# Grouping the 32-column matmuls of a fused attention and gMLP kernel into fewer stretches, and reordering two loads

## The chip, the cores and the metric

The kernel runs on one core of a Trainium2 chip. The metric is the time of one execution in microseconds (us) on that core; lower is better. Three runs of the kernel before gave 208.30, 208.47 and 208.62 us, median 208.47. One further execution was taken by the hardware profiler: its own time is 208.18 us, and its span from the first to the last instruction is 206.5 us. All times inside the kernel are counted from the start of that span.

## The reference

Tokens: S = 2048, width D = 512, all data bf16. The output is the input plus two branches, both fed by the same layer norm:

```
xn  = layernorm(x)                          # over the 512 columns
out = x + attention(xn) + gmlp(xn)

attention: q, k, v = xn @ wqkv              # 32 heads of 16 columns
           logits[s, w] = q[s] . k[s - 2w] / 4,  w = 0..7, masked where s - 2w < 0
           o = softmax over w (logits) applied to v[s - 2w];  result o @ wo
gmlp:      z = gelu(xn @ w_in)              # 1376 columns, split into z1 and z2 (688 each)
           g = w_sp @ layernorm(z2) + b_sp  # w_sp is 2048 x 2048, over the tokens
           result (z1 * g) @ w_out
```

So each token attends to itself and seven earlier tokens, two apart, and the gMLP mixes over all tokens.

## The kernel before, in words

Tokens are handled in 16 tiles of 128. The order of the work on each engine is the order in which the source issues it; no scheduler moves anything. Each engine works through its own queue in order, and so does the DMA queue of SyncE (SP).

**Loads.** x arrives in four blocks of four tiles (`load_x`, L160). The pool `xqp` holds three blocks, so the fourth (L178) has to wait on SP until the four tiles of the first have been normalised. The v weights `wv` (L176) and the small `b16` (L177) are issued between blocks 2 and 3. `a_sb` (L132) is a buffer that holds the softmax weights, written first by `softmax_exp(0)`.

**Layer norm.** VectorE (DVE) computes the statistics of a tile (L185, L186) and normalises it (L190); GpSimd (POOL) does Newton steps for the root. Tiles 0 to 3 are transposed by TensorE (PE). Tiles 4 to 15 go in pairs through the loop at L387, which issues one DMA transpose for each tile (L219) on SP, into `xnT`. Five transposing loads of `w_sp` (`load_wsp`, L343) follow on SP, with `w_z1` (L421) between them.

**First matmul stage, written out by hand, L398 to L479.** Three things are interleaved on PE:
- `z2_tile(i)` (L229): 8 matmuls of 344 columns, then a Gelu on ScalarE (ACT, L234); later `z2_square(i)` on ACT (L238) for the second layer norm.
- `qk_chunk(b, c)` (L260): 8 matmuls of 512 columns for q and k, copied out by ACT (L263).
- `v_pair(d)` (L285) and `reduce_heads(hb, p)` (L310): these two use a *32-column form*. The stationary operand is 128 x 32, and four such matmuls go beside each other to four column positions of the array (`tile_position=(0, 32 * k)`). A `v_pair` is 32 of them, a `reduce_heads` is 16. All other matmuls of this stage fill the array (128 x 128).

`products(hb, p)` (L301, DVE) multiplies q with shifted k; there are two buffers `pr`, so a third product waits for the `reduce_heads` that reads the first. `reduce_heads` sums the 16 columns of each head, ACT scales the result into `lg` (L312), and `softmax_top` (DVE, L317 to L322), `softmax_exp` (ACT, L325) and `softmax_norm` (DVE, L331 to L336) follow once for each half (`hb`) of the tokens.

`z2_stats` (L244) waits for the last square; `z2_norm` (L252) normalises the 16 tiles of z2 on DVE.

A stretch of matmuls in the 32-column form between two others is called an *excursion* here. There are eight: `reduce_heads` with `v_pair` (four times, from L433, L441, L449 and L456), `v_pair(4)` to `v_pair(7)` with `reduce_heads(1, 0)` (from L469), and one `reduce_heads` alone at L519, L523 and L527.

**Mixing stage.** `mix(j)` (L493) is 32 matmuls over `w_sp` and z2; `z1_tile(j)` (L505) is 8 more with a Gelu (L510) on a tile whose padding POOL has cleared (L509); `gate_out(j)` (L515) multiplies on DVE and issues a DMA transpose of the result on SP. Each `mix(j)` also issues the load of `w_sp` for j + 5. From j = 3 on, DVE does the attention's weighted sums (L559 to L568) beside it, at set places.

**Last stage.** PE multiplies with `wo` (L636) and `w_out` (L647, L622), DVE adds x (L651), SP stores.

PSUM: `bank_pair` hands out three double banks in turn, two banks serve `ps_aux` (transposes and head sums).

Of the kernel before, what the change touches and what calls it, by code (L numbers as in the profile page):

```python
# [7 lines left out]
BF16 = mybir.dt.bfloat16  # L8
# [5 lines left out]
P = 128  # L14
S = 2048
D = 512
# [29 lines left out]
def kernel(  # L46
# [20 lines left out]
    SP = nc.sync  # L67

    x2 = A_x.rearrange("b s d -> (b s) d")
# [15 lines left out]
    def bank_pair(name, two=False):  # L85
        turn[0] += 1
        pool = ps_b if turn[0] % 3 == 0 and not two else ps_a
        return pool.tile([P, 2, 512], F32, name=name, tag="mm")
# [43 lines left out]
    a_sb = base.tile([P, W, NB * TG], BF16, name="a_sb")  # L132
# [6 lines left out]
    wv = rpool.tile([P, C, D], BF16, name="wv")  # L139
# [9 lines left out]
    xqp = early.enter_context(tc.tile_pool(name="xqp", bufs=3))  # L149
# [7 lines left out]
    wqkv_r = A_wqkv.rearrange("(k p) f -> p k f", p=P)  # L157
    xq = []

    def load_x(b):  # L160
        t = xqp.tile([P, 4, D], BF16, name="xq")
        SP.dma_start(t[:], x2[b * 4 * P:(b + 1) * 4 * P, :].rearrange("(i p) d -> p i d", p=P))
        xq.append(t)

    x0 = xqp.tile([P, 4, D], BF16, name="xq")
# [4 lines left out]
    SP.dma_start(w_z2[:, 2:4, :], w_in_r[:, 2:4, FH:F])  # L170
    xq.append(x0)
    load_x(1)
    for s in range(2):
        SP.dma_start(wqk[:, :, s, :], wqkv_r[:, :, s * D:(s + 1) * D])
    load_x(2)
    SP.dma_start(wv[:], wqkv_r[:, :, 2 * D:3 * D])  # L176
    SP.dma_start(b16[:], B_b_sp.rearrange("(j p) -> j p", p=P))  # L177
    load_x(3)  # L178
    V.memset(qk[0][:, 1, :, 0:HALO], 0.0)
    V.memset(vp[0:32, :, 0, 0:HALO], 0.0)  # L180

# [1 line left out]
    def ln_stats(i):  # L183
        xs = xq[i // 4][:, i % 4, :]
        V.bn_stats(stats[:, i, :], xs)  # L185
        V.bn_aggr(mv[:, i, :], stats[:, i, :])  # L186

    def ln_apply(i):
        xn = xnp.tile([P, D], BF16, name="xn")
        V.tensor_scalar(xn[:], xq[i // 4][:, i % 4, :], mv[:, i, 0:1], rstd[:, i:i + 1], ALU.subtract, ALU.mult)  # L190
        return xn
# [26 lines left out]
    def transpose_dma(i, xn):  # L218
        SP.dma_start_transpose(xnT[:, :, i * P:(i + 1) * P], xn[:])  # L219

    def z2_start(i):
        pz = bank_pair("pzb")
        for kc in range(C):
            z2_part(i, pz, kc)
        return pz
# [7 lines left out]
    def z2_gelu(i, pz):  # L233
        A.activation(z2[:, i, :].rearrange("p (a b) -> p a b", a=2), pz[:, :, 0:FHALF],  # L234
                     ACT.Gelu_apprx_tanh, accum_out=zsum[:, i:i + 1])

    def z2_square(i):
        A.activation(junk[:], z2[:, i, :], ACT.Square, accum_out=zsq[:, i:i + 1])  # L238

    def z2_tile(i):  # L240
        z2_gelu(i, z2_start(i))
# [13 lines left out]
    def qk_chunk(b, c):  # L255
        tsl = slice(b * 512, (b + 1) * 512)
        pq = bank_pair("pq")
        for s in range(2):
            for kc in range(C):
                PE.matmul(pq[:, s, :], wqk[:, kc, s, c * P:(c + 1) * P], xnT[:, kc, tsl],  # L260
                          start=(kc == 0), stop=(kc == C - 1))
        at = HALO + b % 2 * 512
        A.copy(qk[b // 2][:, :, c, at:at + 512], pq[:])  # L263
# [16 lines left out]
    def v_pair(d2):  # L280
        pv = bank_pair("pv")
        for dd in range(2):
            for kc in range(C):
                for k in range(NG):
                    PE.matmul(pv[32 * k:32 * k + 32, dd, :].rearrange("p (b t) -> p b t", b=NB),  # L285
                              wv_v[:, kc, 2 * d2 + dd, :], xnT_g[:, kc, :, k, :],
                              start=(kc == 0), stop=(kc == C - 1), tile_position=(0, 32 * k))
        A.copy(vp[:, 2 * d2:2 * d2 + 2, :, HALO:HALO + TG],
               pv[:].rearrange("p a (b t) -> p a b t", b=NB))

    def shifted(ap):

        return bass.AP(ap.tensor, ap.offset, [ap.ap[0], [DIL, 2]] + list(ap.ap[1:]))
# [4 lines left out]
    def products(hb, p):  # L298
        pr = prp.tile([P, 2, C, SB], BF16, name="pr")
        off = HALO - DIL * (W - 1 - 2 * p)  # L300
        V.tensor_tensor(pr[:], qk[hb][:, 0, :, HALO:HALO + SB].unsqueeze(1).broadcast_to([P, 2, C, SB]),  # L301
                        shifted(qk[hb][:, 1, :, off:off + SB]), ALU.mult)
        prs[hb, p] = pr

    def reduce_heads(hb, p):
        pr = prs.pop((hb, p))
        pl = ps_aux.tile([P, 2, TG], F32, name="pl", tag="aux")
        for c in range(C):
            for k in range(NG):
                PE.matmul(pl[32 * k:32 * k + 32, :, :], rsel[:, c, :], pr[:, :, c, k * TG:(k + 1) * TG],  # L310
                          start=(c == 0), stop=(c == C - 1), tile_position=(0, 32 * k))
        A.activation(lg[hb][:, 2 * p:2 * p + 2, :], pl[:], ACT.Copy, scale=float(DH) ** -0.5)  # L312

    def softmax_top(hb):
        l = lg[hb]
        if hb == 0:
            V.tensor_tensor(l[0:32, :, 0:HALO], l[0:32, :, 0:HALO], mask[:], ALU.add)  # L317
        m4 = lgp.tile([P, 4, TG], BF16, name="m4", bufs=1)
        V.tensor_tensor(m4[:], l[:, 0:4, :], l[:, 4:8, :], ALU.max)
        V.tensor_tensor(m4[:, 0:2, :], m4[:, 0:2, :], m4[:, 2:4, :], ALU.max)  # L320
        V.tensor_tensor(m4[:, 0, :], m4[:, 0, :], m4[:, 1, :], ALU.max)
        V.tensor_tensor(l[:], l[:], m4[:, 0, :].unsqueeze(1).broadcast_to([P, W, TG]), ALU.subtract)  # L322

    def softmax_exp(hb):
        A.activation(a_sb[:, :, hb * TG:(hb + 1) * TG], lg[hb][:], ACT.Exp)  # L325
# [15 lines left out]
    def load_wsp(j):  # L341
        t = wspp.tile([P, NT, P], BF16, name="wspT")
        SP.dma_start_transpose(t[:], B_w_sp[j * P:(j + 1) * P, :])  # L343
        wsps[j] = t
# [41 lines left out]
    prev = None  # L386
    for g in groups + (None,):  # L387
        if g:
            for i in range(*g):
                ln_stats(i)  # L390
            ln_newton(*g)
        if prev:
            for i in range(*prev):
                transpose_dma(i, ln_apply(i))
        prev = g


# [32 lines left out]
    qk_chunk(2, 1)  # L430
    z2_square(7)
    qk_chunk(2, 2)
    reduce_heads(0, 0)  # L433
    products(0, 2)
    v_pair(0)
    qk_chunk(2, 3)
    z2_tile(8)
    qk_chunk(3, 0)
    z2_square(8)
    qk_chunk(3, 1)  # L440
    reduce_heads(0, 1)  # L441
    products(0, 3)
    v_pair(1)
    qk_chunk(3, 2)
    z2_tile(9)
    qk_chunk(3, 3)
    z2_square(9)
    z2_tile(10)
    reduce_heads(0, 2)  # L449
    products(1, 0)  # L450
    v_pair(2)
    z2_square(10)
    z2_tile(11)
    z2_square(11)
    z2_tile(12)
    reduce_heads(0, 3)  # L456
    softmax_top(0)
    products(1, 1)
    v_pair(3)
    z2_square(12)  # L460
    z2_tile(13)
    z2_square(13)
# [1 line left out]
    z2_square(14)  # L464
    z2_tile(15)
    z2_square(15)


    v_pair(4)  # L469
    z2_stats()  # L470
    z2_norm()
    v_pair(5)
    reduce_heads(1, 0)
    products(1, 2)
    softmax_exp(0)
    v_pair(6)
# [12 lines left out]
    def mix(j):  # L489
        pg = bank_pair("pg", j > 3)  # L490
        for k in range(NT):
            for hh in range(2):
                PE.matmul(pg[:, hh, 0:FHALF], wsps[j][:, k, :], z2[:, k, hh * FHALF:(hh + 1) * FHALF],  # L493
                          start=(k == 0), stop=(k == NT - 1))
        gs = gsp.tile([P, 2, FHALF], BF16, name="gs")
        A.activation(gs[:], pg[:, :, 0:FHALF], ACT.Identity, bias=b_col[:, j:j + 1])  # L496
        if j + 5 < NT:
            load_wsp(j + 5)
        return gs

    def z1_tile(j, gs):
        pz = bank_pair("pz1", j > 3)
        for hh in range(2):
            for kc in range(C):
                PE.matmul(pz[:, hh, 0:FHALF], xnT[:, kc, j * P:(j + 1) * P],  # L505
                          w_z1[:, kc, hh * FHALF:(hh + 1) * FHALF],
                          start=(kc == 0), stop=(kc == C - 1))
        z1 = z1p.tile([P, FPAD], BF16, name="z1")
        G.memset(z1[:, FH:FPAD], 0.0)  # L509
        A.activation(z1[:, 0:FH].rearrange("p (a b) -> p a b", a=2), pz[:, :, 0:FHALF], ACT.Gelu_apprx_tanh)  # L510
        gate[j] = (gs, z1)

    def gate_out(j):
        gs, z1 = gate.pop(j)
        V.tensor_tensor(z1[:, 0:FH], gs[:].rearrange("p a b -> p (a b)"), z1[:, 0:FH], ALU.mult)  # L515
        SP.dma_start_transpose(uT[:, :, j * P:(j + 1) * P], z1[:])

    g0 = mix(0)
    reduce_heads(1, 1)  # L519
    products(1, 3)  # L520
    z1_tile(0, g0)
    g1 = mix(1)
    reduce_heads(1, 2)  # L523
    softmax_norm(0, lgp)
    z1_tile(1, g1)
    gate_out(0)
    reduce_heads(1, 3)  # L527
    softmax_top(1)
    gate_out(1)
    z1_tile(2, mix(2))  # L530
    softmax_exp(1)
    att.close()

# [95 lines left out]
    for pair in range(2):  # L629
# [9 lines left out]
        for jj in (2 * pair, 2 * pair + 1):  # L639
            hb, q = jj // 2, jj % 2  # L640
            for k in range(NG):
                i = 8 * hb + 2 * k + q
# [48 lines left out]
```

## Time and profile before

| what | value |
|---|---|
| median of three runs | 208.47 us |
| profiled execution, its own time | 208.18 us |
| its span | 206.5 us |
| granted clock of PE | 1.00 |
| PE matmul busy | 201.7 us (98%) |
| DVE busy | 166.2 us (81%) |
| ACT busy | 93.6 us (45%) |
| POOL busy | 16.1 us (8%) |

PE's busy time is the union of its matmuls as recorded; these overlap in the record, since the next one starts before the end of the one before is reached. So a busy PE can still hold small gaps between the starts, and the starts are what has to be read. Where the idle time of an engine is named, the last thing it waited for is named with it.

### The profile page before, as it was taken

What the parts mean: (1) busy time and instruction counts of PE and PEld (TensorE: products, weight loads), DVE (VectorE), ACT (ScalarE), POOL (GpSimd) and SP (SyncE); (2) the same over time, 40 slices, a digit from 0 to 9 for tenths busy, and PEclk for the clock granted to TensorE, in tenths of its full rate; (3) what the DMA queues carried; (4) which work ended last, traced back from release to release, by engine and by line L of the source; (5) the groups of instructions that cost most, each with busy time, mean ns of one, the idle gap of its engine ahead of it and who ended that gap; (6) DMA issues with size and microseconds to landing.
All of it is one profiled execution on the core that took longest, in us unless ns stands there. A gap on an engine that the chain in (4) does not pass through costs nothing.

```text
span 206.5 us, 4016 instructions
## 1 busy us (share of the span) xinstructions
PE 201.7 (98%) x1644; PEld 118.3 (57%) x1644; DVE 166.2 (81%) x192; ACT 93.6 (45%) x145; POOL 16.1 (8%) x82
## 2 busy tenths in 40 slices
PE   7999999999999999999999999999999999999994
PEld 4754544545556665566666666666666664444442
DVE  4899939958369699999999999999999955582353
ACT  3777887675689996328633322123333311000000
POOL 5045630000000000000000000000000000000000
PEclk9999999999999999999999999999999999999999
DMA  6996546978000004623975999999544233036432
GB/s 166 318 344 101 103 101 146 236 136 157 3 0 3 3 0 43 134 51 76 174 156 123 231 179 195 217 190 187 122 141 120 45 79 42 25 97 209 115 104 90
DMA packets 67410, 25.63 MB, mean 124 GB/s; under 512 B 57168, under 2 KB 67264, under 8 KB 67264
## 3 DMA queue, kind: packets, MB, share of 16 engines
q1 hardware_dynamic: 67008, 25.24, 57.6%
q8 instruction: 13, 0.21, 0.4%
q10 hardware_dynamic: 384, 0.13, 0.3%
q14 instruction: 5, 0.04, 0.1%
HBM read 9.79 MB, written 2.10 MB: 58 GB/s over the span
## 4 chain that ended last, share of the span: by engine, by line
PE 91%; DVE 3%; DMA 3%; POOL 1%; issue 1%
PE pg L493 36%; PE pq L260 10%; PE po L647 10%; PE pz L505 9%; PE pzb L229 8%; PE pv L285 7%; PE po L636 6%; PE pl L310 4%; DMA xnT<-xn 2%; DVE stats L185 2%; DMA xq<-in_A_x_dram 1%; PE pt L212 1%; PE po L622 1%; DVE xn L190 1%; DVE mv L186 0%
## 5 line engine op out<-in xcount | busy, mean ns | idle before, releaser
L493 PE MATMUL pg<-z,wspT 128*128 128x344 bf16 x512 | 77.3, 309 | 0.0
L493 PEld LDWEIGHTS <-wspT 128*128 128x128 bf16 x512 | 49.9, 98 | 25.2 <-issue 0.8
L301 DVE TENSOR_TENSOR pr<-qk 128x8192 bf16<-128x8192 bf16 x8 | 35.1, 4425 | 6.5 <-PE pl L310 6.5
L496 ACT ACTIVATE gs<-pg,b_col 128x688 bf16<-128x688 f32 x16 | 13.3, 834 | 54.1 <-PE pg L493 54.1
L559 DVE TENSOR_TENSOR pw<-vp,a_sb 128x4096 bf16<-128x4096 bf16 x16 | 36.1, 2285 | 0.0
L651 DVE TENSOR_TENSOR ot<-po,xr 128x512 bf16<-128x512 f32 x15 | 10.2, 689 | 15.2 <-PE po L647 15.1
L260 PE MATMUL pq<-xnT,wqk 128*128 128x512 bf16 x96 | 21.7, 379 | 0.0
L505 PE MATMUL pz<-w_z,xnT 128*128 128x344 bf16 x128 | 21.3, 309 | 0.0
L229 PE MATMUL pzb<-w_z,xnT 128*128 128x344 bf16 x128 | 20.6, 309 | 0.3 <-DMA xnT<-xn 0.3
L647 PE MATMUL po<-wout,uT 128*128 128x512 bf16 x90 | 19.8, 379 | 0.0
L564 DVE TENSOR_TENSOR pw<-pw 128x4096 bf16<-128x4096 bf16 x8 | 18.3, 2288 | 0.1
L229 PEld LDWEIGHTS <-xnT 128*128 128x128 bf16 x128 | 12.0, 98 | 7.7 <-issue 0.8
L505 PEld LDWEIGHTS <-xnT 128*128 128x128 bf16 x128 | 12.4, 98 | 6.8 <-issue 0.8
L260 PEld LDWEIGHTS <-wqk 128*128 128x128 bf16 x96 | 9.2, 98 | 11.1 <-issue 0.8
L647 PEld LDWEIGHTS <-uT 128*128 128x128 bf16 x90 | 8.7, 98 | 11.0 <-issue 0.8
L285 PE MATMUL pv<-xnT,wv 128*32 128x512 bf16 x256 | 14.9, 380 | 0.0
L263 ACT CAST qk<-pq 128x1024 bf16<-128x1024 f32 x12 | 12.1, 1012 | 5.8 <-PE pq L260 5.8
L510 ACT ACTIVATE z<-pz 128x688 bf16<-128x688 f32 x16 | 11.9, 743 | 5.6 <-PE pz L505 4.8
L238 ACT ACTIVATE junk<-z 128x688 bf16<-128x688 bf16 x16 | 12.4, 778 | 0.1
L636 PE MATMUL po<-wo_r,op 32*128 32x512 bf16 x224 | 12.4, 374 | 0.0
L185 DVE BATCH_NORM_STATS2 stats<-xq 128x6 f32<-128x512 bf16 x16 | 10.8, 674 | 1.9 <-DMA xq<-in_A_x_dram 1.9
L234 ACT ACTIVATE z<-pzb 128x688 bf16<-128x688 f32 x16 | 11.8, 736 | 1.0 <-PE pzb L229 1.0
(79 smaller groups left out, 166.7 us busy)
## 6 DMA issues: line engine op xcount, KB each, us to landing
xr<-in_A_x_dram SPq DMA_DIRECT2D x4, 512.0 KB, 4.1
out_dram<-ot SPq DMA_DIRECT2D x15, 128.0 KB, 1.7
wo_r<-in_A_wo_dram SPq DMA_DIRECT2D x4, 448.0 KB, 5.0
xq<-in_A_x_dram SPq DMA_DIRECT2D x3, 512.0 KB, 8.4
wqk<-in_A_wqkv_dram SPq DMA_DIRECT2D x2, 512.0 KB, 7.5
w_z<-in_B_w_in_dram SPq DMA_DIRECT2D x2, 344.0 KB, 4.3
w_z<-in_B_w_in_dram SPq DMA_DIRECT2D x1, 688.0 KB, 7.2
wout<-in_B_w_out_dram SPq DMA_DIRECT2D x1, 640.0 KB, 4.7
```

Of the source, the lines that this page charges most:

```text
L185: V.bn_stats(stats[:, i, :], xs)
L229: PE.matmul(pz[:, hh, 0:FHALF], xnT[:, kc, i * P:(i + 1) * P], w_z2[:, kc, hh * FHALF:(hh + 1) * FHALF], start=(kc == 0), stop=(kc == C - 1))
L260: PE.matmul(pq[:, s, :], wqk[:, kc, s, c * P:(c + 1) * P], xnT[:, kc, tsl], start=(kc == 0), stop=(kc == C - 1))
L285: PE.matmul(pv[32 * k:32 * k + 32, dd, :].rearrange("p (b t) -> p b t", b=NB), wv_v[:, kc, 2 * d2 + dd, :], xnT_g[:, kc, :, k, :], start=( ...
L301: V.tensor_tensor(pr[:], qk[hb][:, 0, :, HALO:HALO + SB].unsqueeze(1).broadcast_to([P, 2, C, SB]), shifted(qk[hb][:, 1, :, off:off + SB]), ...
L493: PE.matmul(pg[:, hh, 0:FHALF], wsps[j][:, k, :], z2[:, k, hh * FHALF:(hh + 1) * FHALF], start=(k == 0), stop=(k == NT - 1))
L496: A.activation(gs[:], pg[:, :, 0:FHALF], ACT.Identity, bias=b_col[:, j:j + 1])
L505: PE.matmul(pz[:, hh, 0:FHALF], xnT[:, kc, j * P:(j + 1) * P], w_z1[:, kc, hh * FHALF:(hh + 1) * FHALF], start=(kc == 0), stop=(kc == C - 1))
L559: V.tensor_tensor(pw[:], shifted(vp[:, :, hb, off:off + P]), a_sb[:, 2 * p:2 * p + 2, osl].unsqueeze(2).broadcast_to([P, 2, DH, P]), ALU.mult)
L564: V.tensor_tensor(pws[p - 1][:], pws[p - 1][:], pw[:], ALU.add)
L636: PE.matmul(pos[jj, k][:], op[32 * k:32 * k + 32, d, jj * P:(jj + 1) * P], wo_r[32 * k:32 * k + 32, d, :], start=(d == 0), stop=((jj, k, d ...
L647: PE.matmul(pos[jj, k][:], uT[:, m, i * P:(i + 1) * P], wout[:, m, :], start=False, stop=(m == MCH - 1))
```

## The change

Three things are moved; no computation is added or left out.

- The eight excursions become four. `reduce_heads(0, 0)` and `(0, 1)` stand together with `v_pair(0)` and `(1)`; `(0, 2)` and `(0, 3)` with `v_pair(2)` and `(3)`; `(1, 0)` and `(1, 1)` stand among `v_pair(5)` to `(7)`; `(1, 2)` and `(1, 3)` come after `mix(2)`. The products on DVE move with the sums that free their buffers, `softmax_top(0)` comes after both `products(1, 0)` and `products(1, 1)`, `z2_tile(11)` and two squares come earlier.
- Block 3 of x is loaded into the first four slots of `a_sb`, without waiting, at the place on SP where `wv` was.
- `wv` is issued on SP inside the loop at L387, after the transposes of tiles 6 and 7.

```diff
     def load_x(b):
-        t = xqp.tile([P, 4, D], BF16, name="xq")
-        SP.dma_start(t[:], x2[b * 4 * P:(b + 1) * 4 * P, :].rearrange("(i p) d -> p i d", p=P))
+
+        t = xqp.tile([P, 4, D], BF16, name="xq") if b < 3 else a_sb[:, 0:4, :]
+        SP.dma_start(t[:] if b < 3 else t, x2[b * 4 * P:(b + 1) * 4 * P, :].rearrange("(i p) d -> p i d", p=P))
         xq.append(t)
...
     load_x(2)
-    SP.dma_start(wv[:], wqkv_r[:, :, 2 * D:3 * D])
+    load_x(3)
     SP.dma_start(b16[:], B_b_sp.rearrange("(j p) -> j p", p=P))
-    load_x(3)
...
                 transpose_dma(i, ln_apply(i))
+            if prev[0] == 6:
+                SP.dma_start(wv[:], wqkv_r[:, :, 2 * D:3 * D])
         prev = g
...
     qk_chunk(2, 2)
-    reduce_heads(0, 0)
-    products(0, 2)
-    v_pair(0)
     qk_chunk(2, 3)
     z2_tile(8)
     qk_chunk(3, 0)
     z2_square(8)
     qk_chunk(3, 1)
+    reduce_heads(0, 0)
     reduce_heads(0, 1)
+    products(0, 2)
     products(0, 3)
+    v_pair(0)
     v_pair(1)
     qk_chunk(3, 2)
     z2_tile(9)
     qk_chunk(3, 3)
     z2_square(9)
     z2_tile(10)
+    z2_square(10)
+    z2_tile(11)
     reduce_heads(0, 2)
+    reduce_heads(0, 3)
     products(1, 0)
     v_pair(2)
-    z2_square(10)
-    z2_tile(11)
+    products(1, 1)
+    softmax_top(0)
     z2_square(11)
+    v_pair(3)
     z2_tile(12)
-    reduce_heads(0, 3)
-    softmax_top(0)
-    products(1, 1)
-    v_pair(3)
     z2_square(12)
...
     reduce_heads(1, 0)
+    reduce_heads(1, 1)
     products(1, 2)
...
     g0 = mix(0)
-    reduce_heads(1, 1)
     products(1, 3)
     z1_tile(0, g0)
     g1 = mix(1)
-    reduce_heads(1, 2)
     softmax_norm(0, lgp)
     z1_tile(1, g1)
     gate_out(0)
+    g2 = mix(2)
+    reduce_heads(1, 2)
     reduce_heads(1, 3)
     softmax_top(1)
     gate_out(1)
-    z1_tile(2, mix(2))
+    z1_tile(2, g2)
     softmax_exp(1)
```

## The prediction, made before the changed kernel was run

> **What bounds the kernel now.** I read part 1 of the page first: PE is busy nearly all the span, so a change must take something out of PE's own line or it gives nothing.
>
> ```profile
> PE 201.7 (98%) x1644; PEld 118.3 (57%) x1644; DVE 166.2 (81%) x192; ACT 93.6 (45%) x145; POOL 16.1 (8%) x82
> ```
>
> Next the chain that ended last: PE again, with one DMA transpose early. Columns are start, length, what, count.
>
> ```profile
> PE 91%; DVE 3%; DMA 3%; POOL 1%; issue 1%
> ...
> 16.41 4.11 DMA xnT<-xn
> 20.52 0.05 issue
> 20.56 2.51 PE pzb L229 x16
> ...
> 36.32 0.98 PE pl L310 x16
> 37.30 1.73 PE pv L285 x32
> 39.03 1.83 PE pq L260 x8
> ...
> 51.18 1.73 PE pq L260 x8
> ...
> 69.14 0.86 PE pl L310 x16
> 70.01 3.45 PE pv L285 x64
> 73.46 4.77 PE pg L493 x32
> ...
> 94.31 4.67 PE pg L493 x32
> ```
>
> The same work has two prices. 16 head sums that follow full-array matmuls take 0.98 us, 16 that follow v products take 0.86. Eight q/k matmuls after an excursion take 1.83 us, after other full-array matmuls 1.73; a mix takes 4.77 after one and 4.67 otherwise. Between head sums and v products nothing is added (37.30, 1.73 for eight groups of four). So it is the change of form that costs, once in and once out.
>
> The timelines of PE, DVE and SP then give the waits:
>
> ```profile
> 18.91 1.34 PE L229 MATMUL pzb<-w_z,xnT 128*128 128x344 bf16 x8
> 20.56 2.51 PE L229 MATMUL pzb<-w_z,xnT 128*128 128x344 bf16 x16 [0.31 <-DMA xnT<-xn]
> ```
>
> ```profile
> 64.45 4.42 DVE L301 TENSOR_TENSOR pr<-qk 128x8192 bf16<-128x8192 bf16 x1
> 68.78 0.17 DVE L244 TENSOR_SCALAR zmean<-zsum 128x16 f32<-128x16 f32 x1
> ```
>
> PE waits once after its start-up, for the transpose of tile 5; and z2_stats on DVE starts as its last product ends (68.78) and ACT's last square (68.63), so both chains are late together.
>
> **Part 1, eight excursions to four.** From start to start, a 512-column matmul follows the one before it after 0.216 us and a 344-column one after 0.146. At each of the eight entries the first 32-column matmul starts 0.310 (or 0.239) after the last full one: 0.094 too much. At each of the eight exits it is 0.312 in place of 0.216: 0.096. The step after each is 0.010 longer. Together 0.21 us for an excursion, the same for all eight (the entry by v products at 65.46 costs 0.05 more, and stays). Four go: 4 x 0.21 = **-0.84 us**, on PE, on the path. The matmuls themselves are the same in number.
>
> The Trainium skill, "TensorEngine Tiling (Array Packing)", Key Properties, says that changing the tiling mode drains the array. Read as a wait for the last matmul's recorded end (0.379 us after its start, against a pitch of 0.216), a switch would cost 0.163 and eight switches -1.30 us; the rows show the next form starting 0.07 us before that end, so I keep the rows.
>
> **What the new order makes late.** I laid the durations of the rows in the new order, each start being the latest of its engine's last, its inputs, and its PSUM bank or buffer.
>
> - *DVE, first half.* products(0, 2) waited for the head sum at 36.3; it now waits for the one at 42.1 and starts at 43.1 instead of 39.9, (0, 3) follows without a wait and ends at 51.9 (50.9 before). Their head sums are due at 54.4 and 55.3: 2.5 us spare. products(1, 0) starts at 55.5 (55.2 before), (1, 1) ends at 64.2, softmax_top(0), 2.9 us, at 67.2. The order before ended both at 68.8, because softmax_top then waited 1.9 us for ACT. So z2_stats is no longer held by DVE but by ACT's last square.
> - *ACT.* From z2_tile(11) on it works without a break; moving square 10 and Gelu 11 ahead fills the breaks that stood before the copies of v_pair (0.90 and 0.53 us). The last square ends at 68.0 (68.6 before), the first normalised tile of z2 comes out about 0.7 us earlier.
> - *mix(0).* One more head sum (1, 1) stands ahead of it, +0.86, against what was saved by then; it starts at 73.2 to 73.4, as now. The 16 normalisations take 6.0 us, the mix 4.67, so the last one decides: it had 0.4 us to spare (77.4 against 77.8), and gets about 1.0. If that cover goes, PE waits microsecond for microsecond.
> - *Second half.* softmax_top(1) now waits for a head sum after mix(2): its scores are ready at 92.1, DVE is there at 91.5. So DVE begins the weighted sums at 95.2 as now, while PE is over 1 us further. Behind softmax_top(1) are gate_out(1) and softmax_exp(1). The exp ends at 98.2, and gs(3) behind it on ACT is 0.8 us late; the bank that it holds is next wanted over 2 us later. At the end of the mixing DVE waits 2.90 us for ACT at 171.0; that shrinks to about 1.6 and hides this. After it DVE waits 4.0 us for PE at 177.7, so the tail moves with PE.
> - *SP.* The load for mix(7) is now issued ahead of the transpose of gate_out(1); both had to wait for work before 96. It landed at 101.5 and is wanted at 116.
>
> No term on the path: 0.
>
> **Part 2, the loads.** Block 3 of x takes the place of wv: same size, same rows of 1 KB, so 6.26 issued and 15.29 landed, where it now lands at 18.05. Its users come at 20.97: no direct gain. But half a megabyte less stands ahead of the transposes. Transposes of tiles 4 and 5 took 3.84 and 4.11 us to land, eight of the ten after them 2.43 to 2.60 and none above 2.67. Tile 5 landed at 20.52; PE could have begun it at 20.09 (last start 19.942 + 0.146). With 2.7 us from its issue at 16.41 it lands at 19.1, 1 us early. Gain by starts 20.564 - 20.088 = **-0.48 us** (the 0.31 of the row is counted from a recorded end). What is late next: tile 6 (landed 20.99, wanted from 21.25) and tile 7 (22.17, wanted 22.4), with 0.2 us or more. No gain and a full gain are the ends of this term: the reason to doubt stands under rival A.
>
> wv is issued on SP at about 20.9, ahead of the transposes of tiles 8 to 15; an issue of such a load took 0.5 us (wqk) to 1.9 (wv into a full queue), and its data 1.5 us (the second wqk landed 1.5 after the first). Tile 11 landed at 27.43; qk_chunk(2, 0) wants it at 30.5: 3.0 us spare against 2.0. The w_sp loads behind them land by 51.1 and are wanted at 73. wv itself is wanted at 43.8. Cost 0. a_sb is written by softmax_exp at 73.8, long after the last reader of x at 29.3.
>
> **Sum.** -0.84 - 0.48 = -1.32. From the profiled execution's 208.18 that gives 206.86; the median of the runs is 0.29 higher, 208.47, and gives 207.15. I say 207.1.
>
> **Rivals.**
>
> *A. The wait for tile 5 stays.* The trace's DMA records speak for it: block 3's data ended at 16.2, just as the first transpose's began (16.25), so they hardly overlap. An instruction load of 16 KB (queue q8) held one of the DMA engines from 16.06 to 17.17; its share of tile 4 was only done at 17.97, and SP's issue of tile 5 was held until 18.23 (1.81 us, others 1.22). Transposes in the mixing stage that met such a load took 4.2 and 4.3 us, the others some 2.75. If that load comes at the same moment, nothing is won. Against it: its start fell just where block 3's data ran out, and PE had begun 181 instructions, where most later loads come at 154 to 176 modulo 256; so it may have queued behind the data, and then comes up to 1.5 us earlier. Time: 208.18 - 0.84 = 207.34, by the median 207.63.
>
> *B. The price is not in the form.* If the 0.1 us belongs to the first use of a stationary operand after others and pairing only moves it, only -0.48 stays: 207.70 to 207.99. Against it: the v products right after head sums pay nothing.
>
> *C. Slower: wv among the transposes.* If each of tiles 8 to 11 behind wv goes as tile 5 did, SP needs 0.6 more for each (2.4), wv's issue 0.5 to 1.9, and the last lands 1.6 late: 4.5 to 5.9 us, where 3.0 are spare. PE waits 1.5 to 2.9 at qk_chunk(2, 0): 206.86 + 1.5 to 2.9 = 208.4 to 209.8, by the median 208.7 to 210.1. It is slower than before once tile 11 is 4.4 us late. Against it: at 20 to 30 us the DMA engines carry about 100 GB/s, and 350 at 8 to 15.
>
> *D. A cover is missing in the middle*, mostly mix(0) behind z2_norm: each us beyond about 1 (ACT) counts fully; with 2.3 us late the time is as before, 208.2 to 208.5.
>
> **Chances.** Both gains 0.57, A 0.28, B 0.05, C 0.06, D 0.04. About 0.2%, 0.4 us, is what a measurement of this kernel tells from no change. The forecast, A and most of B are faster by more: 0.90; D and the rest of B the same: 0.05; C slower: 0.05. The range goes from 206.6 (the forecast from the profiled execution, with 0.3 less for a mix(0) or tile 4 that also starts earlier) to 207.8 (A by the median, with the scatter of 0.16 of the runs): 0.85 lie in it. C and D are left out.
>
> **What would show it.** Right: four switches in and four out before the last stage, each still 0.094 to 0.096 us over the pitch; head sums of 0.86 in second place; PE goes from z2_tile(4) to z2_tile(5) without a gap, tile 5 landing near 19; mix(0) 4.77 without a wait; DVE's wait before the last gate shrinks to about 1.6 us. Wrong: tile 5 landing again at 20.5 (A); 0.1 us at the start of each group within an excursion (B); a wait at qk_chunk(2, 0) for xnT (C); a mix(0) longer than 4.8 us (D).

## The result, and the profile after

The changed kernel takes 206.90 us (median of 4 runs, 206.84 to 206.97); the kernel before, measured beside it, 208.38 (4 runs, 208.25 to 208.62). The ratio is 0.9928, interval 0.9911 to 0.9945, so about 1.5 us less, between 1.15 and 1.85. Forecast were 1.32 us. The profiled execution takes 206.84 us with a span of 205.1 (before: 208.18 and 206.5).

The page of the changed kernel, parts 1 and 4:

```profile
PE 199.7 (97%) x1638; PEld 118.6 (58%) x1644; DVE 166.2 (81%) x192; ACT 93.4 (46%) x145; POOL 16.1 (8%) x82
...
PE 94%; DMA 3%; SPq 1%; issue 0%; DVE 0%
```

PE is even more of the chain than before (94% for 91%). Six of its 1644 matmuls have no record, so the chain below has a few holes in which PE was at work. The chain of waits of the changed kernel (start, length, what, count):

```profile
2.70 5.33 DMA w_z<-in_B_w_in_dram
...
19.20 3.61 PE pzb L229 x24
...
38.96 3.45 PE pq L260 x16
42.41 1.84 PE pl L310 x32
44.25 3.45 PE pv L285 x64
...
54.76 1.84 PE pl L310 x32
56.60 3.45 PE pv L285 x64
60.06 4.77 PE pzb L229 x32
64.83 3.61 PE pv L285 x64
68.44 1.73 PE pl L310 x32
70.17 3.45 PE pv L285 x64
73.62 4.77 PE pg L494 x32
...
90.06 1.84 PE pl L310 x32
91.90 1.27 PE pz L506 x8
93.17 4.67 PE pg L494 x32
```

Four excursions are left, at 42.4, 54.8, 64.8 and 90.1. 32 head sums take 1.84 us: 0.98 for the first sixteen and 0.86 for the second, so the second pays no entry. The transpose of tile 5 is gone from the chain. mix(0) starts where it did (73.62 for 73.46, with one more head sum ahead of it), and the mix that started at 94.31 now starts at 93.17: from here on PE is 1.14 us ahead.

PE's timeline of the changed kernel shows all three of z2_tile(4) to (6) as one stretch of 24 matmuls, where it broke after eight for tile 5:

```profile
19.14 3.67 PE L229 MATMUL pzb<-w_z,xnT 128*128 128x344 bf16 x24
```

And DVE's timeline of the changed kernel, at the places that the prediction named:

```profile
43.44 8.76 DVE L301 TENSOR_TENSOR pr<-qk 128x8192 bf16<-128x8192 bf16 x2 [3.79 <-PE pl L310]
55.85 8.76 DVE L301 TENSOR_TENSOR pr<-qk 128x8192 bf16<-128x8192 bf16 x2 [3.65 <-PE pl L310]
...
67.49 0.17 DVE L244 TENSOR_SCALAR zmean<-zsum 128x16 f32<-128x16 f32 x1
...
68.01 0.18 DVE L246 SCALAR_TENSOR_TENSOR zvar<-zsq,zvar 128x16 f32<-128x16 f32 x1
...
70.81 6.00 DVE L252 TENSOR_SCALAR z<-z,zmean,zrstd 128x688 bf16<-128x688 bf16 x16
...
92.58 0.69 DVE L319 TENSOR_TENSOR m<-lg 128x1024 bf16<-128x1024 bf16 x1 [0.98 <-ACT lg L312]
...
169.87 0.52 DVE L516 TENSOR_TENSOR z<-gs,z 128x688 bf16<-128x688 bf16 x1 [1.36 <-ACT z L511]
```

The products come in twos behind long waits that cost PE nothing. z2_stats starts at 67.49 (68.78 before) and the normalising at 70.81 (71.47 before). ACT's last square ends at 67.98, and L246, which reads it, starts at 68.01: ACT is now what z2_stats waits for.

**A steadier measure than the whole time.** The first loads land at slightly different times in each execution: in 14 traces z2_tile(4) starts between 18.59 and 19.32 us, and in this pair the changed kernel is 0.23 us late there (19.14 for 18.91). What follows repeats almost exactly. So for each profiled execution I also take the stretch from the start of z2_tile(4) to the start of the last mixing matmul: 149.76 us before, 148.40 after, **-1.37** by the unrounded starts.

The span itself is 1.32 us shorter (206.45 to 205.13): the late start takes 0.23 off the gain, and the ending, from the last mixing matmul on, is 0.18 shorter (37.78 to 37.60) and gives most of that back. This ending has two lengths: 37.78 to 37.81 us before and in e2, e3, e7, e8 and e9, 37.58 to 37.60 in the other eight traces. The last store lands 36.74 to 36.76 after the last mixing matmul in all of them; what differs is ACT's closing DRAIN instruction after it (37.43 to 37.46 against 37.14 to 37.16). What sets it isn't shown, and the stretch leaves it out. Some later runs are also 2 us off the rest of their own series; where that is so, the range is given.

### The profile page after: what moved, and what is told of

Same layout as the page of the kernel before. It is cut to its first block, busy times and chain, and to the rows that moved or that the text cites. A ratio compares the mean times of both kernels' runs of the same rounds, so it can differ in the third digit from the quotient of the medians.

```text
span 205.1 us, 4013 instructions
## 1 busy us (share of the span) xinstructions
PE 199.7 (97%) x1638; PEld 118.6 (58%) x1644; DVE 166.2 (81%) x192; ACT 93.4 (46%) x145; POOL 16.1 (8%) x82
## 4 chain that ended last, share of the span: by engine, by line
PE 94%; DMA 3%; SPq 1%; issue 0%; DVE 0%
PE pg L494 36%; PE pq L260 10%; PE po L648 9%; PE pz L506 9%; PE pzb L229 9%; PE pv L285 7%; PE po L637 6%; PE pl L310 4%; PE pq L272 3%; DMA w_z<-in_B_w_in_dram 3%; PE po L623 1%; SPq L170 0%; PE pt L212 0%; SPq L169 0%; DVE ot L625 0%
## 5 line engine op out<-in xcount | busy, mean ns | idle before, releaser
L652 DVE TENSOR_TENSOR ot<-po,xr 128x512 bf16<-128x512 f32 x15 | 10.2, 689 | 15.2 <-PE po L648 15.1
L648 PE MATMUL po<-wout,uT 128*128 128x512 bf16 x88 | 19.3, 379 | 0.3 <-issue 0.3
L285 PEld LDWEIGHTS <-wv 128*32 128x32 bf16 x256 | 9.4, 139 | 4.6 <-issue 0.3
```

What stands on the lines that cost most here:

```text
L648: PE.matmul(pos[jj, k][:], uT[:, m, i * P:(i + 1) * P], wout[:, m, :], start=False, stop=(m == MCH - 1))
```

## The experiments

All were timed in five rounds against the kernel before, on three chips. "Stretch" is the measure above, against the 149.76 of the kernel before; it comes from one profile each.

| kernel | median us (lowest to highest, runs) | before, same chip | ratio (interval) | stretch |
|---|---|---|---|---|
| e0 changed, again | 206.74 (206.58-207.03, 5) | 207.98 | 0.9935 (0.9922-0.9949) | -1.37 |
| e1 loads only | 207.60 (207.19-207.70, 8) | 207.98 | 0.9976 (0.9966-0.9986) | -0.48 |
| e2 excursions only | 207.43 (207.04-207.77, 6) | 207.98 | 0.9971 (0.9958-0.9985) | -0.75 |
| e3 changed, wv early | 207.18 (207.01-207.74, 5) | 207.98 | 0.9963 (0.9949-0.9977) | -0.91 |
| e4 changed, block 3 in the pool | 206.60 (206.36-206.73, 6) | 208.18 | 0.9920 (0.9906-0.9934) | -1.37 |
| e5 changed, in turn | 206.66 (206.33-206.84, 6) | 208.18 | 0.9924 (0.9909-0.9938) | -1.37 |
| e6 changed, eight again | 207.70 (207.28-209.68, 12) | 208.18 | 0.9997 (0.9973-1.0020) | -0.31 |
| e7 changed, block 3 later | 207.84 (207.48-209.46, 12) | 208.18 | 0.9994 (0.9976-1.0011) | -0.42 |
| e8 before, longer warm-up | 207.83 (207.56-209.83, 12) | 208.28 | 0.9992 (0.9967-1.0017) | -0.48 |
| e9 e2, longer warm-up | 207.88 (206.53-209.15, 12) | 208.28 | 0.9978 (0.9950-1.0006) | -0.87 |
| e10 changed, DVE late | 211.01 (209.43-211.51, 6) | 208.28 | 1.0113 (1.0076-1.0149) | +3.16 |
| e11 changed, longer warm-up | 206.75 (206.49-207.35, 6) | 208.28 | 0.9930 (0.9904-0.9956) | -1.37 |

The theory was that of the prediction: 0.21 us for each of four excursions, and 0.48 for the wait. The rivals were that the price belongs to something else than the form (B), and that the wait goes for another reason than the loads, or needs the load into a_sb.

### e0: the changed kernel again, beside its parts

No edit.

> The changed kernel unaltered, on the same chip as the three parts, for a direct comparison: 1.3 to 1.6 us under the kernel before by every theory.

-1.24 us by the medians, the stretch again -1.37. On this chip the kernel before has the lowest of its medians (207.98, against 208.18 to 208.38 elsewhere), so the differences of e0 to e3 by medians come out small.

### e1: the loads alone

The kernel before with the loads of the changed one:

```diff
-        t = xqp.tile([P, 4, D], BF16, name="xq")
+        t = xqp.tile([P, 4, D], BF16, name="xq") if b < 3 else a_sb[:, 0:4, :]
...
-    SP.dma_start(wv[:], wqkv_r[:, :, 2 * D:3 * D])
+    load_x(3)
     SP.dma_start(b16[:], B_b_sp.rearrange("(j p) -> j p", p=P))
-    load_x(3)
...
+            if prev[0] == 6:
+                SP.dma_start(wv[:], wqkv_r[:, :, 2 * D:3 * D])
```

> The loads alone: block 3 of x early into a_sb, wv after the transposes of tiles 6 and 7, with the eight excursions of before. Theory (two separate gains, 0.48 us from the wait for tile 5 and 0.84 from four excursions): 0.4 to 0.6 us under the kernel before, tile 5 landing near 19.1 and no wait of PE for it, eight excursions at 0.21 us. Rival (the gain is all in the new order of the middle, by what it does for ACT and z2_norm): as before, within 0.2 us; or the 0.48 is given back at mix(0), where the last normalised tile of z2 had 0.4 us to spare: then mix(0) is longer than 4.77 us and only 0.4 or less is left.

-0.38 us by the medians, the stretch -0.48. PE's timeline of this kernel:

```profile
18.78 3.67 PE L229 MATMUL pzb<-w_z,xnT 128*128 128x344 bf16 x24
```

No break, and all eight excursions as before: the loads take the wait away by themselves, and nothing else. mix(0) starts at 72.78 in the trace and doesn't wait for z2, though the 16 normalisations leave only 0.3 us (they end at 76.85, the last is wanted by the 31st mixing matmul at 77.17).

### e2: the excursions alone

The changed kernel with block 3 in the pool and wv where it was before:

```diff
-        t = xqp.tile([P, 4, D], BF16, name="xq") if b < 3 else a_sb[:, 0:4, :]
+        t = xqp.tile([P, 4, D], BF16, name="xq")
...
-    load_x(3)
+    SP.dma_start(wv[:], wqkv_r[:, :, 2 * D:3 * D])
     SP.dma_start(b16[:], B_b_sp.rearrange("(j p) -> j p", p=P))
+    load_x(3)
...
-            if prev[0] == 6:
-                SP.dma_start(wv[:], wqkv_r[:, :, 2 * D:3 * D])
```

> The order of the middle alone: four excursions, with the loads of before. Theory: 0.75 to 1.0 us under the kernel before, the wait for tile 5 stays (tile 5 landing near 20.5, PE 0.48 us late by starts). Rival (excursions cost nothing by themselves; the loads do it): within 0.2 us of before. If both parts lean on each other, this run and the one of the loads alone do not add up to the whole change (1.5 us).

-0.55 us by the medians, less than expected. PE's timeline of this kernel:

```profile
19.24 1.34 PE L229 MATMUL pzb<-w_z,xnT 128*128 128x344 bf16 x8
21.02 2.51 PE L229 MATMUL pzb<-w_z,xnT 128*128 128x344 bf16 x16 [0.45 <-DMA xnT<-xn]
```

By starts the wait for tile 5 is 0.61 here (it could have begun at 19.24 + 8 x 0.146 = 20.41, and began at 21.02), 0.13 more than in the kernel before. So of the stretch's -0.75 the excursions make -0.88, and the wait gives 0.13 back. In the other order, on top of the loads, the medians of e1 and e0 say -0.86, and the stretches -0.88. The stretch shows no smaller price; why the medians of e2 say 0.2 less than its stretch isn't shown, beyond the low median of the kernel before on this chip.

### e3: wv early again

The changed kernel with wv ahead of the transposes once more, behind b16:

```diff
     SP.dma_start(b16[:], B_b_sp.rearrange("(j p) -> j p", p=P))
+    SP.dma_start(wv[:], wqkv_r[:, :, 2 * D:3 * D])
...
-            if prev[0] == 6:
-                SP.dma_start(wv[:], wqkv_r[:, :, 2 * D:3 * D])
```

> The changed kernel with wv issued right after block 3 of x and b16, so again ahead of the transposes; block 3 still goes into a_sb without a wait. As much data stands ahead of the transposes as before. Theory (the half megabyte ahead of the transposes made the wait): the wait comes back, tile 5 lands later than 20.1, 0.3 to 0.6 us above the changed kernel, about 0.9 under before; the 16 KB instruction load starts again near 16 us, as the plain data run out. Rival (it was the wait on SP for a free x buffer, or the landing of block 3 itself, at 18.05): no wait, same time as the changed kernel within 0.15.

+0.44 us over e0 by the medians, +0.46 in the stretch. PE's timeline:

```profile
20.36 2.51 PE L230 MATMUL pzb<-w_z,xnT 128*128 128x344 bf16 x16 [0.28 <-DMA xnT<-xn]
```

The wait is back though block 3 has landed at 15.38, so it is not the place of block 3 that counts but half a megabyte ahead of the transposes, or what comes with it (see e8).

### e4: block 3 without a_sb

Block 3 in the pool, where it has to wait on SP for the first four tiles; only wv is moved:

```diff
-        t = xqp.tile([P, 4, D], BF16, name="xq") if b < 3 else a_sb[:, 0:4, :]
+        t = xqp.tile([P, 4, D], BF16, name="xq")
...
-    load_x(3)
     SP.dma_start(b16[:], B_b_sp.rearrange("(j p) -> j p", p=P))
+    load_x(3)
```

> The changed kernel with block 3 of x in its pool buffer again, issued after b16 behind the wait for the first block's tiles, so that only wv is moved. Theory (what counts is that wv no longer stands ahead): same as the changed kernel within 0.15 us, tile 5 landing near 19.1. Rival (the load into a_sb, free of the wait on SP, is what helps): 0.3 to 0.6 us above the changed kernel, with a wait for tile 5.

Like the changed kernel: 206.60 us, stretch -1.37, no wait for tile 5. Block 3 is issued at 8.93 and lands at 15.58, early enough. The load into a_sb is worth nothing; the later wv is what helps.

### e5: head sums and v products in turn

The changed kernel, its excursions kept, but within each the kinds alternate:

```diff
     reduce_heads(0, 0)
-    reduce_heads(0, 1)
     products(0, 2)
-    products(0, 3)
     v_pair(0)
+    reduce_heads(0, 1)
+    products(0, 3)
     v_pair(1)
```

(and likewise around `v_pair(2)` and `v_pair(6)`).

> The changed kernel with head sums and v products in turn inside three of the four excursions, so that the stationary operand changes between rsel and wv five times more (nine for four), while the number of excursions stays four. Theory (the price is in the change of form): same as the changed kernel within 0.15 us. Rival (the price belongs to the first use of other stationary operands): about 0.1 us for each added change, 0.4 to 0.5 us above it.

206.66 us, stretch -1.37: the same. The chain of waits of this kernel:

```profile
41.86 0.98 PE pl L310 x16
42.84 1.73 PE pv L285 x32
44.57 0.86 PE pl L310 x16
45.43 1.73 PE pv L285 x32
47.16 1.83 PE pq L260 x8
```

Three changes of kind inside, and only the first head sums (0.98) and the q/k matmuls after the last (1.83) pay. Rival B falls: changing the stationary operand within the form costs nothing.

### e6: eight excursions again

The pairs kept, but `v_pair(0)` to `(3)` moved out, each between full-array matmuls:

```diff
-    v_pair(0)
-    v_pair(1)
     qk_chunk(3, 2)
+    v_pair(0)
     z2_tile(9)
+    v_pair(1)
     qk_chunk(3, 3)
...
-    v_pair(2)
...
-    v_pair(3)
     z2_tile(12)
+    v_pair(2)
     z2_square(12)
     z2_tile(13)
+    v_pair(3)
```

> The changed kernel with v_pair(0) to (3) taken out of the first two excursions and put one by one between full-array groups: eight excursions again, at other places than before, head sums still in pairs. Theory: 0.21 us for each of four more, and 0.05 more for each that is entered by v products: 0.84 to 1.05 us above the changed kernel, without a new wait. Rival (the gain of the new order is not in the number of excursions but in what it does for ACT and DVE): under 0.4 us above it.

+1.04 us over e5 and +1.10 over e4 by the medians, +1.06 in the stretch. (Two of its 12 runs took 209.6 and 209.7 us, hence the wide interval of its ratio.) The chain of waits of this kernel:

```profile
42.25 1.84 PE pl L310 x32
44.09 1.83 PE pq L260 x8
45.92 1.88 PE pv L285 x32
47.80 1.27 PE pzb L229 x8
49.08 1.89 PE pv L285 x32
50.96 1.83 PE pq L260 x8
```

Each part pays for itself: v products 1.88 for 1.73, q/k 1.83 for 1.73, z2 1.27 for 1.17. An entry by v products costs 0.045 more than one by head sums (its second step is 0.262 in place of 0.216), so 4 x (0.22 + 0.045) = 1.06: the number of excursions, and by what they are entered, sets the stretch, to 0.01 us.

### e7: block 3 among the transposes

The changed kernel with block 3 issued after the transposes of tiles 4 and 5, still into `a_sb`, so that almost no data are left when these run:

```diff
-    load_x(3)
...
+            if prev[0] == 4:
+                load_x(3)
```

> The changed kernel with block 3 of x issued after the transposes of tiles 4 and 5, so that a further half megabyte no longer stands ahead of them. Its first reader, the statistics of tile 12, stands at 21 us. Theory (the 16 KB instruction load comes when the plain data ahead of it run out): the load starts about 1.5 us earlier than 14.1, near 12.6, and tiles 4 and 5 land as in the changed kernel, so nothing is gained at PE; block 3 may hold up tiles 6 and 7 by 0.5 to 2 us, where 0.2 are to spare: 0 to 1.5 us slower than the changed kernel. Rival (the instruction load is asked for at a set place in PE's queue and starts there): it stays near 14.1.

+1.2 us over e4 by the medians, +0.95 in the stretch, and its ending is 0.21 longer. PE's timeline of this kernel:

```profile
18.68 2.51 PE L228 MATMUL pzb<-w_z,xnT 128*128 128x344 bf16 x16
21.96 1.34 PE L228 MATMUL pzb<-w_z,xnT 128*128 128x344 bf16 x8 [0.78 <-DMA xnT<-xn]
```

Tile 5 is in time; now tile 6 is late, behind block 3: issued at 18.16, landed at 21.91, 3.76 us where 2.5 are usual. In these runs half a megabyte on SP held up the transposes right behind it at each of its three places, by 0.5 to 2 us: with wv early, tiles 4 and 5 took 3.0 to 4.1 us (before, e2, e3, e9; but 2.5 in e8), here tile 6 takes 3.76, and with wv late tile 8 took 4.2 to 4.5. The run was also to tell when PE's instruction load (the 16 KB of rival A) comes. The first loads' data ended by 12.8 us, and it came at 13.72. So my idea in the prediction, that it waits only until the data run out, falls in that form: without them it comes at about PE's 160th instruction, matmuls and weight loads counted (160 to 169 in eight traces), and where data are still thick, later (174 in e3, 176 in e2, 181 before).

### e8, e9, e11: the instruction load or the data?

In all traces so far the wait for tile 5 went together with an instruction load after 15.1 us, and this with data that ended late. To move the load alone, PE's warm-up, which touches no data of the kernel, was made of 30 matmuls of 128 columns in place of 17 of 256, so that its instruction count runs 26 ahead (13 matmuls and their weight loads). The same edit on the kernel before (e8), on e2 (e9) and, as a control, on the changed kernel (e11):

```diff
-    spin(17)
+    for _ in range(30):
+        PE.matmul(idle[:, 0, 0:P], ones[:, 0:P], ones[:, 0:P], start=True, stop=True)
```

> The kernel before, with its 17 warm-up matmuls of 256 columns replaced by 30 of 128 columns: 26 more PE instructions ahead of everything, so that PE's 16 KB instruction load, which the traces show at the 160th to 181st instruction, is asked for some 2.8 us earlier. As much data stands ahead of the transposes as before. Theory L (the instruction load holds one DMA engine while tile 4 is transposed): it starts before 14.5 us, is over before the transposes, tile 5 lands before 20.1 and the wait of 0.45 to 0.6 us for it goes: 0.3 to 0.6 us faster than before. Theory D (the data ahead of the transposes do it by themselves): the wait stays, same as before within 0.2. If the load is held until the data run out, near 16 us, nothing is told apart.

> The order of the middle alone (four excursions, loads of before) with the same 30 warm-up matmuls. Theory L: the wait for tile 5 goes without any change of the loads, as fast as the changed kernel within 0.2 us, 1.3 to 1.6 under before. Theory D: as the order of the middle alone, 0.5 to 0.9 under before.

> The changed kernel with the 30 warm-up matmuls, the control for the two runs that move the instruction load: it has no wait for tile 5 to lose. Theories L and D: same as the changed kernel within 0.15 us. If it is faster or slower by more, the warm-up matmuls do something of their own, which is to be taken off the other two.

PE's timeline of e8, the kernel before with this edit:

```profile
18.94 3.67 PE L230 MATMUL pzb<-w_z,xnT 128*128 128x344 bf16 x24
```

and of e9:

```profile
20.39 2.51 PE L230 MATMUL pzb<-w_z,xnT 128*128 128x344 bf16 x16 [0.33 <-DMA xnT<-xn]
```

In e8 the load began at 14.96 in place of 16.06, with wv still early, and the wait is gone: stretch -0.48, the same as by moving wv. In e9 it began only at 15.21, and the wait of 0.49 stayed. e11 is as the changed kernel: its load began at 13.83, 2.5 us after PE's 160th instruction (11.36) and about when the data thinned out (289 GB/s between 13.5 and 13.75, 82 between 14.0 and 14.25). So the edit made the load due earlier, but didn't make it come earlier by as much. As times, e8 and e9 say nothing: both series are spread over 2.3 to 2.6 us (of e9 six runs lie at 206.5 to 207.5 and six at 208.2 to 209.2, for which I have no cause).

Over all 14 traces, the wait for tile 5 is there where the load began at 15.19 or later (the kernel before, e2, e3, e9), and absent where it began at 14.96 or earlier.

But the bulk data ended earlier in e8 as well: between 15.25 and 15.5 us the DMA engines moved 119 GB/s, against 205 in e3, 201 in e9 and 270 before. And up to some 36 us e8 and e9 hold the same instructions; one execution had the wait and the other not. So whether the load or the data ahead of it holds the transposes is not settled by these runs. What they show is that with wv ahead of the transposes four traces of five have the wait for tile 5, and without it none of nine.

### e10: is the cover at mix(0) real?

To make DVE late ahead of z2_stats by one product, `products(1, 1)` is repeated into the same buffer with the same values; the added work is the 4.4 us of one instruction:

```diff
     v_pair(4)
+    V.tensor_tensor(prs[1, 1][:], qk[1][:, 0, :, HALO:HALO + SB].unsqueeze(1).broadcast_to([P, 2, C, SB]),
+                    shifted(qk[1][:, 1, :, HALO - DIL * (W - 3):HALO - DIL * (W - 3) + SB]), ALU.mult)
```

> The changed kernel with products(1, 1) done twice on DVE, the second time (4.4 us, same values) right ahead of z2_stats: it tells how much cover the middle has. By the changed kernel's rows z2_stats may come about 2 us later before ACT's root waits for it, and the last normalised tile (76.7) stands 1.2 us before mix(0) wants it: 1.0 to 2.2 us slower than the changed kernel, at mix(0). Rival (DVE's chain has no cover there): 4.4 us slower. Rival (DVE is far off the path): no change within 0.2.

+4.26 us over e11: far outside what was expected, by a flaw of the experiment. `reduce_heads(1, 1)` reads that buffer, so PE waited there and not at mix(0). PE's timeline of this kernel, and its chain of waits:

```profile
71.58 1.05 PE L310 MATMUL pl<-pr,rsel 128*32 128x512 bf16 x16 [2.65 <-DVE pr L470]
```

```profile
72.63 5.14 PE pv L285 x64
77.77 4.77 PE pg L496 x32
```

The wait is 2.8 us by starts. Then the 64 v products take 5.14 us in place of 3.45: 1.69 more. Together 4.5, which is the stretch (3.16 + 1.37 = 4.53). The windows of this kernel say why, PEclk being the clock granted:

```profile
71.60:73.60 2.00, 2.00 (x32) 1.17 (x35) 1.44 (x7) 1.46 (x3) 0.00 (x0) 0.77 0.03 8
73.60:75.60 2.00, 2.00 (x24) 0.95 (x20) 2.00 (x7) 1.98 (x3) 0.00 (x0) 0.50 0.00 0
75.60:77.60 2.00, 2.00 (x36) 1.19 (x28) 2.00 (x7) 1.99 (x3) 0.00 (x0) 0.88 0.00 0
77.60:79.60 2.00, 2.00 (x17) 1.29 (x14) 2.00 (x5) 1.77 (x2) 0.00 (x0) 1.00 0.00 0
```

The clock fell to half, shortly after PE had begun again. It did so in four of the six runs (210.99 to 211.51 us): those have a mean clock of 0.992, while the two others, at 209.43 and 209.70, have 1.000 and 0.999 and lie 2.7 and 2.9 us over e11, about the wait alone. mix(0), now at 77.77, had z2 3.3 us before it needed it. So how much mix(0) has to spare was not measured by taking it away; it is read from the rows only.

## Why the prediction was right, step by step

**Part 1, four excursions fewer: right, 0.04 us too small.** Foretold -0.84, the stretches give -0.88 (e1 to the changed kernel, 149.28 to 148.40). The 0.04 is the exit, which the prediction took too small by 0.010 us each time: within the form, four matmuls start 0.206 after the last of the four before, so an exit at 0.312 costs 0.106, while the prediction compared it with 0.216 and got 0.096. With that an excursion is 0.094 + 0.106 + 2 x 0.010 = 0.22 and four are -0.88; the rows that the prediction shows say the same (0.98 - 0.86 and 1.83 - 1.73).

All entries and exits of the changed kernel before its last stage still start 0.310 (0.239 after z2 or mixing matmuls) and 0.312 after the matmul before, and e5 and e6 show from both sides that it is the change of form that costs: the same excursions with their kinds mixed take the same time, more excursions with the same matmuls take more. The Trainium skill, "TensorEngine Tiling (Array Packing)", Key Properties, read as a full drain would have made it -1.30 us; the runs agree with the rows. What inside the change costs is not told apart: in the kernel before, the weight load of a full-array matmul starts a whole matmul ahead of it (35.73 for the one at 35.95), at the entry at 36.26 and the exit at 38.96 only with its matmul, and no run separates this from the change of form itself.

**Part 2, the wait for tile 5: right in its size and in moving wv; what held the transposes stays open.** Foretold -0.48, the stretch of e1 gives -0.48. Tile 5 landed at 19.16 (19.1 foretold), 2.48 us after its issue. Whether it was the data or the instruction load of rival A, e8 and e9 don't tell. What was not needed is the first half of this part: block 3 can stay in the pool (e4). e7 shows what was foretold as late next, tile 6, with its price.

**What the new order makes late: right, zero on the path.** The rows of DVE above: products(0, 2) at 43.44 (43.1 foretold), z2_stats at 67.49 (67.2), normalising 0.66 us earlier (0.7); ACT's last square ended at 67.98 (68.0); mix(0) at 73.55 (73.2 to 73.4), 4.77 long and without a wait. By the same working as in e1 it has 1.1 us to spare (76.81 against 77.94; about 1.0 foretold). The kernel before had 0.3 (77.47 against 77.78, not the 0.4 of the prediction), and e1 ran with 0.3. DVE's wait for softmax_top(1) is 0.98 and not the 0.6 (92.1 - 91.5) that was worked out, and that before the last gate 1.36 and not 1.6; DVE starts the weighted sums at 95.67, 0.4 later than before (95.26, where it was to be equal), 0.23 of it the late start of this execution; the wait before the last gate took it up.

**The rivals.** A (the wait stays) didn't happen in the changed kernel, but it was close: the instruction load came at 14.14, ahead of the transposes, and in e0, the same kernel, at 14.87, where e3 and e9 with a load at 15.2 have the wait. The prediction had no row that decided this; the nine traces without wv ahead decide it, as none of them has the wait. The reason given against it was half right: the load does come earlier when the data end earlier, but with the warm-up of before never before PE's 160th instruction. B falls by e5. C (wv makes tile 11 late): wv was issued at 20.69 in 0.57 us, and tile 11 landed at 27.78, against 30.72 wanted; the transposes of tiles 8 to 10 took 4.37, 3.57 and 2.81 us where 2.5 are usual, so they are held up, and the 2.9 us of cover took it. D didn't happen.

**Sum.** -1.32 foretold; -1.37 in the stretch, -1.5 (1.15 to 1.85) by the runs of the result and -1.24 and -1.53 by the medians of e0 and e11. Of the 0.05 between forecast and stretch 0.04 is part 1. The shorter ending gives a further 0.18, for which the prediction has no term ("the tail moves with PE"): stretch and ending make -1.55, which fits the medians of e4, e5 and e11 on two other chips (-1.58, -1.52, -1.53). What sets the ending stays open. The rest is the scatter of starts, which a forecast can't have.

No run points to a version that is faster than the changed kernel: e4, e5 and e11 equal it.

## What to carry to other kernels

Look for one kind of matmul with two durations in the same profile: the difference, read from start to start, is the price of what stands ahead of it; here it was had by grouping. Compare each step with the step that it replaces: an exit from a form with the step inside that form. In this kernel a bulk load delayed the transposes right behind it in the same queue at all three places tried (in all executions but that of e8), so it belongs where their results aren't awaited, and the next result in line is what to look at. For effects under half a microsecond compare a stretch between two events of the busy engine, not only the whole time: here the first repeated to 0.01 us and the second to some tenths.

## What the runs showed of the hardware that was not expected

- A wait of PE in the middle of the kernel can cost more than its length. In e10 3.03 us lay between the starts of two matmuls, and 1.1 us after PE had begun again eight steps took 0.427 us in place of 0.216, for 3.4 us, +1.7 us. Two of the six runs of this kernel kept a mean clock of 1.000 and 0.999 and were 1.3 to 2.1 us shorter than the others. The Trainium skill, "TensorE: Matmul & The Clock Gate", Part 1, says that the clock is halved after at least one idle window of about 3.4 us and that the window is 3413 ns long; the 3.4 us at half clock agree with this length, but here a shorter pause was enough, in four runs of six. The waits of 0.5 to 0.94 us in the other kernels left the clock at 1.00.
- PE's instruction load shows among the DMA packets: in the kernel before one of 16 KB held a DMA engine from 16.06 to 17.17. With 26 more PE instructions in the warm-up (e8) it began 1.1 us earlier; but between two executions of the changed kernel its start differs by 0.73 (14.14 and 14.87), so one execution of each can't give all of this to the warm-up.
